# Gated linear attention: the first 512 tokens in plain float32, batch 0's softmax over q on TensorE, and a new order of steps

## The chip, the cores and the metric

The kernel runs on one core of one Trainium2 chip. The metric is the device time of one execution in microseconds (us), median of the runs shown; lower is better.

## The reference

Batch B = 8, heads H = 8, sequence S = 576, head width D = 64, so the model width is C = 512. Cut to what matters:

```
q_s = softmax(q, over the 64 channels of a head)          # one group per token and head
k_s = softmax(k, over the 576 tokens)                      # one group per head and channel
kv  = k_s^T v                                              # 64 x 64 per head
x   = q_s kv                                               # 576 tokens x 512 channels per batch
gate = sigmoid(conv_w, 5 causal taps over the tokens, of x)
out = ((gate * (x @ w_val)) @ w_out)                       # both weights 512 x 512
```

`w_val`, `conv_w` and `w_out` come as 64-bit floats, and the kernel itself turns their two 32-bit words into float32.

## The kernel before, in words

The whole kernel is one list of steps, `ORDER`, written out by hand; each name in it is a function, and every engine's queue holds its instructions in just that order (PE is TensorE, DVE is VectorE, ACT is ScalarE, POOL is GpSimd; SP issues every DMA). A letter at the end of a step (`a`, `v`, `p`) says which engine does it: ACT, DVE or POOL. A step whose input isn't there holds up everything behind it on its engine.

The weights: `load_words i` brings one slab of 128 columns (0 to 3 of `w_val`, 4 to 7 of `w_out`, 8 the taps); `field`, `part`, `scaled`, `signed`, `joined` make float32 of it (L235 to L254); `w_high` rounds it to float32r, and `w_low` takes the rest (L256 to L262).

Per batch b: `load_q`, `q_max`, `q_sub`, `q_exp`, `q_sum`, `q_mul` are the softmax over q with tokens on the partitions (L377 to L393); `q_turn` transposes it on PE (L399), and `q_turned` copies it to `qT`, channels on the partitions. Batches 0 to 2 go this way; later ones load q transposed and take a log-sum through memory. `k_top`, `k_raise`, `k_turn`, `k_turned` are the softmax over k for batches 0 and 1. `kv b` (40 calls of a float32 matmul in 128x64 and 64x64 tiles, L463) and `kv_norm` give `kvd`; `attend b g` (8 calls, 288 columns each, two token halves by two head pairs by two row halves, so four 64x64 tiles of the array at once, L492) writes x of two channel blocks p = 2g, 2g+1 to PSUM. There are two such PSUM tiles (tag `x`, two banks each), so `attend b 1` waits until every reader of `attend b 0` is done. The readers are `first` and four `tap`s per block (the convolution; on DVE in one instruction, L528, or as an ACT product and a POOL add, L532 and L533), `x_high` (x rounded to float32r, into `xx`) and `x_low` (the rest, L514). `sigmoid` is a tanh on ACT.

Then the 4608 tokens are cut in nine tiles of 512, i = 0 to 8; tile 0 is the first 512 tokens of batch 0. `value i m` is 128 rows of x @ w_val in 12 float32r matmuls of 512 columns (three products of high and low halves for each of four blocks, L549); `gated` multiplies with the gate, `g_high` and `g_low` split the product, and `project i t` is another 12 matmuls (L573); `store` evicts and writes. Four `value` and four `project` steps stand for each tile, 72 in all:

```
for kb in range(NB):
    hi, lo = T["xx", i, kb][:, :C], T["xx", i, kb][:, C:]
    for j, (a, z) in enumerate(((wl, hi), (wh, hi), (wh, lo))):
        nc.tensor.matmul(ps, a[:, kb, ms], z, start=(kb == 0 and j == 0), stop=(kb == NB - 1 and j == 2))
```

Other PSUM results use four banks of tag `mm`. The functions of the diff follow.

Of the kernel before, what the change touches and what calls it, by code (L numbers as in the profile page):

```python
# [37 lines left out]
PITCH = 2340  # L38
GAPS = {'w': 64, 'pair': 96, 'gp': 96}

ORDER = [step.strip() for step in """
    load_words 8, field 8, part 8 a, load_q 0 r, scaled 8 v, signed 8, q_max 0 r, q_sub 0 3 v, q_sub 0 2 p, q_exp 0 r,
    joined 8 p, load_q 0 l, q_max 0 l, load_words 0, field 0, q_sub 0 0 v, scaled 0 a, load_q 1 a, part 0 a,
    load_words 3, part 3 a, q_sub 0 1 v, signed 0, joined 0 p, load_kc 0 2, q_sum 0 r, load_ident, field 3, scaled 3
    a, load_kc 0 0, load_kc 0 3, load_kc 0 1, load_words 4, q_max 1 a, w_high 0 a, q_exp 0 l, load_words 2, k_top 0 3,
    k_raise 0 3, k_top 0 1, k_raise 0 1, k_turn 0 1, q_mul 0 2 p, q_mul 0 3 p, q_tail_turn 0, k_top 0 0, k_top 0 2,
    k_raise 0 2, k_raise 0 0, k_turn 0 2, w_low 0 p, q_sum 0 l, k_turned 0 2 a, k_tail_turn 0, q_tail_turned 0 a,
    field 2, load_v 0, field 4, scaled 4 a, q_sub 1 1 v, q_sub 1 3 p, q_mul 0 1 v, part 2 a, signed 4, k_turn 0 0,
    signed 3, load_kc 1 1, k_turned 0 0 a, q_sub 1 0 p, q_sub 1 2 p, scaled 2 a, signed 2, k_turn 0 3, joined 2 p,
    k_turned 0 1 a, k_tail_turned 0 a, k_turned 0 3 a, kv 0, load_kc 1 0, q_exp 1 a, q_mul 0 0 v, q_turn 0 0,  # L50
    load_words 1, w_high 2 p, q_turned 0 0 a, k_top 1 1, kv_norm 0 0 a, q_turn 0 1, q_turned 0 1 a, field 1, scaled 1
    a, q_sum 1 a, joined 3 p, w_high 3 a, q_turn 0 2, q_turned 0 2 a, w_low 2 p, attend 0 0, first 0 1 a, x_high 0 1 0
    a, load_q 5 a, first 0 0 a, q_turn 0 3, kv_norm 0 1 a, x_high 0 0 1 a, load_kc 1 2, k_top 1 2, k_raise 1 2, tap 0
    1 0 v, w_low 3 p, x_high 0 1 1 a, q_mul 1 0 p, part 4 a, joined 4 p, tap 0 0 1 a, load_words 5, load_words 6, part
    5 a, w_high 4 a, field 5, scaled 5 a, field 6, signed 1, tap 0 1 1 v, w_low 4 p, q_turned 0 3 a, q_mul 1 1 p,
    k_raise 1 1, q_mul 1 3 p, load_kc 1 3, k_top 1 3, x_low 0 1 0, x_low 0 1 1, part 1 a, q_mul 1 2 v, q_turn 1 0, tap
    0 1 3 a, tap 0 0 0 v, load_q 2 a, x_high 0 0 0 a, load_words 7, q_max 2 a, field 7, q_sub 2 3 p, k_turn 1 2,
    q_turned 1 0 a, load_km 2 0, scaled 6 a, x_low 0 0 0, k_turned 1 2 a, tap 0 0 3 v, x_low 0 0 1, q_turn 1 1, k_turn
    1 1, k_raise 1 3, q_turn 1 3, k_turned 1 1 a, k_turn 1 3, load_km 2 1, tap 0 0 2 v, sigmoid 0 0, signed 5, joined
    5 p, load_v 1, q_sub 2 0 p, scaled 7 a, q_tail_turn 1, q_turned 1 1 a, q_tail_turned 1 a, load_qc 5, w_high 5 a,  # L60
    k_top 1 0, k_raise 1 0, tap 0 1 2 v, k_peak 2 0, attend 0 1, k_peak 2 1, x_high 0 2 0 a, k_turn 1 0, load_k 4,
    x_high 0 3 0 a, x_low 0 3 0, first 0 2 a, k_turned 1 0 a, x_high 0 3 1 a, q_turn 1 2, q_turned 1 2 a, k_tail_turn
# [586 lines left out]
```

## Time and profile before

| | |
|---|---|
| median of 3 runs | 297.15 us (296.78 to 297.23) |
| profiled execution | 297.07 us, span 295.3 us |
| PE busy | 261.6 us, 89% of the span |
| DVE busy | 244.8 us, 83% |
| ACT busy | 192.4 us, 65% |
| POOL busy | 195.8 us, 66% |

A row of a view gives a start, a busy time and the instruction's tile names (output <- inputs). Busy times of neighbours overlap a little, so the cost of an instruction in a full queue is the distance from its start to the next start. Matmuls overlap by more, and for them only distances of starts count. The granted clock is the share of TensorE's full 2.4 GHz.

### The profile page before, as it was taken

The numbers are of one execution on the slowest core, as the hardware profiler recorded it, in microseconds if no ns is written. First come the engines' busy times: TensorE is split into PE (matmuls) and PEld (weight loads), VectorE is DVE, ScalarE is ACT, GpSimd is POOL, SyncE is SP. The second block draws the span as 40 slices with busy tenths as digits, with TensorE's granted clock in tenths as the row PEclk, the third lists the DMA queues.
The fourth block names the chain that finished last, engine by engine and source line by source line (L and its number), as shares of the span: only waits on it lengthen the run. The fifth ranks groups of instructions, "written<-read, shape, count | busy, mean of one in ns | idle before, by whom it ended". The sixth has DMA issues, their size and how long they took to land.

```text
span 295.3 us, 5125 instructions
## 1 busy us (share of the span) xinstructions
PE 261.6 (89%) x1854; PEld 202.9 (69%) x1854; DVE 244.8 (83%) x412; ACT 192.4 (65%) x299; POOL 195.8 (66%) x184
## 2 busy tenths in 40 slices
...
GB/s 230 386 406 406 356 252 366 385 285 271 269 283 232 220 259 211 299 198 243 228 199 169 159 309 296 188 108 271 237 127 228 2 71 78 29 2 0 107 90 88
DMA packets 21801, 63.06 MB, mean 214 GB/s; under 512 B 3472, under 2 KB 7696, under 8 KB 18448
## 3 DMA queue, kind: packets, MB, share of 16 engines
...
## 4 chain that ended last, share of the span: by engine, by line
PE 80%; DVE 8%; ACT 3%; POOL 3%; DMA 2%; issue 1%; SPq 0%; DVEq 0%; POOLq 0%; ACTq 0%
PE val L549 32%; PE out L573 31%; PE kv L463 7%; PE x L492 6%; DMA words<-in_w_val 2%; PE kps L326 2%; DVE gate L528 2%; PE qps L399 1%; DVE g L556 1%; DVE gl L564 1%; DVE kpk L282 1%; DVE qm L377 1%; ACT qT L194 1%; POOL gl L564 1%; ACT gate L520 1%
## 5 line engine op out<-in xcount | busy, mean ns | idle before, releaser
L549 PE MATMUL val<-xx,w_val_hi 128*128 128x512 f32 x288 | 88.9, 390 | 0.0
L533 POOL TENSOR_TENSOR gate<-gate,far 128x572 f32<-128x572 f32 (+3 forms) x46 | 58.7, 1280 | 33.7 <-ACT far L532 32.1
L528 DVE SCALAR_TENSOR_TENSOR gate<-x,cw,gate 128x574 f32<-128x574 f32 (+3 forms) x82 | 65.3, 806 | 0.8
L549 PEld LDWEIGHTS val<-xx,w_val_hi 128*128 128x128 f32 x288 | 54.1, 188 | 11.0
L573 PE MATMUL out<-w_out_hi,gl 128*128 128x512 f32 x144 | 56.7, 394 | 1.4 <-DVE gl L564 1.1
L549 PE MATMUL val<-xx,w_val_lo 128*128 128x512 f32 x144 | 57.7, 400 | 0.3 <-DVE g L556 0.3
L573 PE MATMUL out<-w_out_lo,gh 128*128 128x512 f32 x144 | 57.4, 399 | 0.2 <-ACT gh L194 0.2
L573 PE MATMUL out<-w_out_hi,gh 128*128 128x512 f32 x144 | 56.2, 390 | 0.0
L532 ACT ACTIVATE far<-x,cw 128x572 f32<-128x572 f32 (+3 forms) x46 | 33.5, 747 | 15.2 <-DVE gate L528 7.2
L564 POOL TENSOR_TENSOR gl<-g,gh 128x512 fp32r<-128x512 f32 x26 | 28.8, 1113 | 14.3 <-ACT gh L194 9.5
L380 POOL TENSOR_TENSOR q<-q,qm 128x576 f32<-128x576 f32 x27 | 32.6, 1226 | 5.9 <-DVE qm L377 5.9
L556 DVE SCALAR_TENSOR_TENSOR g<-gate,val 128x128 f32<-128x128 f32 (+7 forms) x64 | 27.4, 447 | 8.9 <-PE val L549 5.9
L549 PEld LDWEIGHTS val<-xx,w_val_lo 128*128 128x128 f32 x144 | 27.0, 188 | 9.5 <-issue 3.1
L573 PEld LDWEIGHTS out<-w_out_hi,gl 128*128 128x128 f32 x144 | 27.0, 188 | 9.3 <-DVE gl L564 1.9
L573 PEld LDWEIGHTS out<-w_out_lo,gh 128*128 128x128 f32 x144 | 27.0, 188 | 9.0 <-issue 3.1
L514 DVE TENSOR_TENSOR xx<-x,xx 128x512 fp32r<-128x512 f32 (+7 forms) x64 | 27.5, 449 | 5.4 <-ACT xx L194 4.0
L573 PEld LDWEIGHTS out<-w_out_hi,gh 128*128 128x128 f32 x144 | 27.0, 188 | 5.3
L200 ACT ACTIVATE o<-out 128x512 f32<-128x512 f32 x25 | 14.8, 599 | 21.6 <-PE out L573 21.6
L194 ACT CAST xx<-x 128x448 fp32r<-128x448 f32 (+7 forms) x39 | 15.7, 414 | 14.7 <-PE x L492 7.9
L538 ACT ACTIVATE gate<-gate 128x576 f32<-128x576 f32 x32 | 21.5, 684 | 5.8 <-DVE gate L528 2.8
L326 PE MATMUL kps<-ident,kc 128*128 128x128 f32 x32 | 8.0, 408 | 18.3 <-ACT kc L214 18.3
L520 ACT ACTIVATE gate<-x,cw 128x576 f32<-128x576 f32 x23 | 16.9, 746 | 9.7 <-DVE xx L196 5.4
...
## 6 DMA issues: line engine op xcount, KB each, us to landing
...
```

What stands on the lines that cost most here:

```text
L380: engine(e).tensor_sub(groups(b, h), groups(b, h), wide(T["qm", b], h))
L463: nc.tensor.matmul(to, kk[r, o:o + D], vv[r, c * H + n], start=(c == 0), stop=(c == 4))
L514: nc.vector.tensor_sub(xx(i, p)[:, n], T["x", b, p][:, t], xx(i, p)[:, o].bitcast(F32))
L520: nc.scalar.activation(a, x, AF.Copy, scale=w)
L528: nc.vector.scalar_tensor_tensor(out=a, in0=x, scalar=w, in1=a, op0=ALU.mult, op1=ALU.add)
L532: nc.scalar.activation(part, x, AF.Copy, scale=w)
L533: nc.gpsimd.tensor_add(a, a, part)
L538: nc.scalar.activation(T["gate", b, p], T["gate", b, p], AF.Tanh, scale=0.5)
L549: nc.tensor.matmul(ps, a[:, kb, ms], z, start=(kb == 0 and j == 0), stop=(kb == NB - 1 and j == 2))
L556: nc.vector.scalar_tensor_tensor(out=T["g", i, m][:, o], in0=T["gate", b, m][:, t], scalar=1.0, in1=T["val", i, m][:, o], op0=ALU.add, op1 ...
L564: engine(e).tensor_sub(T["gl", i, m], T["g", i, m], T["gh", i, m].bitcast(F32))
L573: nc.tensor.matmul(ps, a, z[:, kb], start=(kb == 0 and j == 0), stop=(kb == NB - 1 and j == 2))
```

## The change

- The constant `ident` becomes 258 columns wide: the identity, its negative, and two columns that sum 64 rows each (`pairs_of`). It is loaded first.
- Batch 0's softmax over q: `q_lift` brings raw q across with a matmul by the identity, `q_lower` subtracts the row maxima (the maxima spread over 64 columns, times the negative identity, accumulated in the same PSUM tile), `q_raise` is the exponential out of PSUM into `qT`; `q_total` sums over channels by a matmul with two columns, `q_rate` inverts, `q_wide` spreads the inverses over channels by matmul, `q_scale` multiplies. This takes the place of `q_sub`, `q_exp`, `q_sum`, `q_mul`, `q_turn`, `q_turned` for batch 0. These PSUM tiles use tag `x`.
- `heat` and `warm` are transposes of the identity whose results nobody reads.
- Tile 0: `value 0 m` and `project 0 t` use the float32 weights (`wp`) and float32 x and g in 4 matmuls each, in place of 12 float32r ones; `x_low` of tile 0 and `g_high`, `g_low` of tile 0 go.
- The weights stand in 18 slots of tag `w` (8 `wp`, 8 `wh`, 8 `wl` in all), slabs of `w_out` are now rows, not columns, and the `w_high`, `w_low` steps come later in the order. `q_sum` no longer inverts; `q_inverse` does for batches 1 and 2.
- `GAPS` changes, and `ORDER` is new throughout.

The diff, cut to its core (the new order up to the first projections; the rest of the orders left out):

```diff
+PITCH = 2340
+GAPS = {'pair': 16, 'gp': 112}
...
-PITCH = 2340
-GAPS = {'w': 64, 'pair': 96, 'gp': 96}
+WS = 18
...
+    load_ident, heat 0 0, heat 1 0, load_words 8, field 8, scaled 8 a, signed 8, part 8 p, load_q 0 l, q_max 0 l, heat
+    2 16, heat 3 0, load_q 0 r, q_max 0 r, q_lift 0 1, q_lower 0 1, load_q 1 a, q_lift_end 0, q_lower_end 0,
+    load_words 7, q_raise 0 1, load_kc 1 1, q_lift 0 3, q_lower 0 3, q_lift 0 0, q_max 1 a, q_raise_end 0, field 7,
+    scaled 7 a, load_kc 0 2, k_top 0 2, k_top 1 1, q_lower 0 0, q_lift 0 2, q_lower 0 2, part 7 a, q_sub 1 1 p, q_sub
+    1 0 p, k_raise 0 2, q_sub 1 2 p, k_raise 1 1, joined 8 p, load_kc 0 1, k_top 0 1, q_sub 1 3 p, q_raise 0 0,
+    load_words 4, part 4 a, field 4, scaled 4 a, load_kc 0 0, load_kc 0 3, k_top 0 0, k_raise 0 0, signed 7, load_kc 1
+    2, q_raise 0 2, k_top 1 2, q_raise 0 3, warm 0 8, q_total 0 0, q_total 0 1, q_total 0 2, load_words 3, k_top 0 3,
+    q_total 0 3, q_total_end 0, signed 4, field 3, q_exp 1 a, load_words 2, field 2, k_turn 0 0, k_turned 0 0 a,
+    scaled 2 p, warm 1 4, warm 2 8, load_kc 1 0, q_rate 0, q_wide 0 0, k_raise 0 1, k_turn 0 1, k_raise 0 3, scaled 3
+    a, k_tail_turn 0, part 2 a, q_wide 0 1, q_sum 1 a, joined 4 p, warm 3 0, load_words 0, field 0, warm 4 8, q_scale
+    0 0, part 0 a, q_inverse 1 a a, k_turned 0 1 a, q_scale 0 1, load_kc 1 3, k_top 1 3, signed 3, scaled 0 a, k_turn
+    0 3, load_v 0, part 3 a, q_mul 1 3 p, load_words 6, field 6, k_turn 0 2, k_turned 0 2 a, load_km 2 0, k_raise 1 3,
+    q_wide_end 0, k_tail_turned 0 a, k_top 1 0, k_turned 0 3 a, load_words 5, q_scale_end 0, q_wide 0 2, q_scale 0 2,
+    kv 0, k_peak 2 0, k_raise 1 0, joined 3 p, k_raise 1 2, kv_norm 0 0 a, field 5, scaled 5 a, w_high 3 a, kv_norm 0
+    1 a, load_q 2 a, q_wide 0 3, q_scale 0 3, q_mul 1 0 p, signed 0, q_mul 1 1 p, warm 5 4, attend 0 0, first 0 1 a,
+    first 0 0 a, q_mul 1 2 p, q_turn 1 1, signed 2, load_km 3 1, joined 2 p, load_words 1, tap 0 1 2 v, tap 0 0 2 a,
+    load_km 2 1, x_high 0 0 1 a, tap 0 1 0 a, q_max 2 a, q_sub 2 0 p, tap 0 0 0 v, joined 0 p, k_tail_turn 1, k_turn 1
+    0, k_turned 1 0 a, q_turned 1 1 a, x_high 0 1 0 a, q_tail_turn 1, x_low 0 0 1, q_tail_turned 1 a, tap 0 1 3 v,
+    scaled 6 a, k_turn 1 2, tap 0 0 1 v, part 1 a, load_v 1, load_v 3, k_tail_turned 1 a, x_high 0 1 1 a, x_low 0 1 1,
+    k_turn 1 3, k_turned 1 3 a, tap 0 0 3 v, k_turned 1 2 a, x_high 0 0 0 a, k_turn 1 1, k_turned 1 1 a, q_turn 1 2,
+    tap 0 1 1 v, q_turn 1 0, q_turned 1 0 a, q_sub 2 2 p, w_high 4 a, signed 6, signed 5, part 5 a, q_turn 1 3, part 6
+    a, q_turned 1 3 a, field 1, joined 5 p, attend 0 1, first 0 3 a, x_high 0 2 0 a, joined 6 p, scaled 1 a, kv 1,
+    k_peak 2 1, tap 0 3 2 v, load_q 3 a, load_v 2, first 0 2 a, x_high 0 3 0 a, kv_norm 1 0 a, tap 0 2 3 v, tap 0 2 1
+    v, value 0 2, sigmoid 0 0, value 0 0, k_row 2, q_sub 2 3 p, q_sub 2 1 p, q_exp 2 a, signed 1, x_high 0 2 1 v,
...
     def w_high(i, e="a"):
-        copied(e, W[i // NB][0][:, :, slab(i)], T["f", i].bitcast(F32).rearrange("p (k c) -> p k c", k=NB))
+        copied(e, weight("wh", i, F32R), T["wp", i].bitcast(F32))
...
+    def heat(k, n):
+        for j in range(n):
+            nc.tensor.transpose(zone(0, 0)[:, j % 2 * P:j % 2 * P + P], ident, ident)
+
+    def q_lift(b, p):
+        for c in range(4):
+            o = c * C + p * P
+            nc.tensor.matmul(zone(b, p)[:, c * P:(c + 1) * P], T["q", b][:, o:o + P], ident, start=(c == 0), stop=False)
...
+    def over_heads(to, t, o, by, start, stop):
+        for h in range(2):
+            w = t[:, o + h:o + h + 1].broadcast_to([P, D])
+            nc.tensor.matmul(to[h * D:(h + 1) * D], w, by, start=start, stop=stop)
+
+    def q_lower(b, p):
+        for c in range(4):
+            over_heads(zone(b, p)[:, c * P:(c + 1) * P], T["qm", b], c * H + 2 * p, minus, False, c == 3)
...
+    def q_raise(b, p):
+        exp(across(b)[:, p, :MAIN], zone(b, p))
...
+    def q_total(b, p):
+        for c in range(4):
+            o = c * H + 2 * p
+            nc.tensor.matmul(totals(b)[:, o:o + 2], across(b)[:, p, c * P:(c + 1) * P], pairs_of, start=True, stop=True)
...
+    def q_wide(b, p):
+        for c in range(4):
+            over_heads(zone(b, p, "rate")[:, c * P:(c + 1) * P], T["qs", b], c * H + 2 * p, ident, True, True)
...
+    def q_scale(b, p):
+        t = across(b)[:, p, :MAIN]
+        nc.vector.tensor_mul(t, t, zone(b, p, "rate"))
...
     def value(i, m):
         ps = T["val", i, m] = bank(f"val_{i}_{m}")
...
+        if i == 0:
+            w = cols(T["wp", m].bitcast(F32))
+            for kb in range(NB):
+                nc.tensor.matmul(ps, w[:, kb], T["xx", i, kb][:, :C], start=(kb == 0), stop=(kb == NB - 1))
+            return
...
     def project(i, t):
         ps = T["out", i, t] = bank(f"out_{i}_{t}")
...
+            if i == 0:
+                nc.tensor.matmul(ps, T["g", i, kb][:, ts], T["wp", NB + kb].bitcast(F32), start=(kb == 0), stop=(kb == NB - 1))
+                continue
```

## Rows read from the trace of the kernel before

**Rows 1.** The page, busy time of each engine with share and instructions.
```profile
PE 261.6 (89%) x1854; PEld 202.9 (69%) x1854; DVE 244.8 (83%) x412; ACT 192.4 (65%) x299; POOL 195.8 (66%) x184
```

**Rows 2.** The page, the chain that ended last, shares by engine.
```profile
PE 80%; DVE 8%; ACT 3%; POOL 3%; DMA 2%; issue 1%; SPq 0%; DVEq 0%; POOLq 0%; ACTq 0%
```

**Rows 3.** Windows: stretch, length, busy of PE, PEld, DVE, ACT, POOL; clock, DMA, GB/s.
```profile
0.00:18.29 18.29, 0.00 (x0) 0.00 (x0) 13.49 (x21) 7.98 (x11) 8.07 (x13) 1.00 0.90 327
18.29:30.50 12.21, 11.97 (x134) 9.43 (x134) 11.94 (x22) 10.98 (x20) 6.52 (x7) 1.00 1.04 408
30.50:38.89 8.39, 0.33 (x2) 0.14 (x1) 8.31 (x16) 7.96 (x17) 6.78 (x7) 0.72 0.71 265
38.89:44.42 5.53, 5.53 (x26) 5.20 (x26) 5.50 (x10) 4.94 (x10) 4.39 (x4) 0.50 0.91 338
44.42:49.05 4.63, 3.41 (x29) 1.93 (x28) 4.63 (x6) 4.46 (x10) 4.63 (x6) 1.00 0.96 356
49.05:87.98 38.93, 38.77 (x335) 30.01 (x337) 38.30 (x57) 33.41 (x56) 35.41 (x36) 1.00 0.86 305
87.98:291.31 203.33, 201.55 (x1337) 156.17 (x1336) 162.69 (x286) 122.05 (x178) 130.05 (x118) 1.00 0.58 168
```

**Rows 4.** The chain in order of time: start, length, what, with the matmul records.
```profile
52.08 2.83 PE kv L463 x80
...
60.58 1.13 PE x L492 x16
...
247.07 22.20 PE val L549 x96
```

**Rows 5.** Timeline of PE: start, busy time, instruction and how many.
```profile
28.42 1.50 PE L492 MATMUL x<-qT,kvd 64*64 64x288 f32 x16
...
64.49 1.04 PE L399 MATMUL qps<-ident,q 128*128 128x128 f32 x8
65.36 0.38 PE L413 MATMUL qtps<-ident,q 128*128 128x128 f32 x2
```

**Rows 6.** Timeline of DVE, a first wait and a stretch without idle time.
```profile
4.96 1.35 DVE L377 TENSOR_REDUCE qm<-q 128x18 f32<-128x1152 f32 x1 [1.75 <-DMA q<-in_q]
...
37.42 2.53 DVE L377 TENSOR_REDUCE qm<-q 128x36 f32<-128x2304 f32 x1
39.88 0.41 DVE L242 TENSOR_SCALAR e<-words 128x512 f32<-128x512 f32 x1
40.22 0.68 DVE L514 TENSOR_TENSOR xx<-x,xx 128x512 fp32r<-128x512 f32 x1
40.82 0.80 DVE L528 SCALAR_TENSOR_TENSOR gate<-x,cw,gate 128x575 f32<-128x575 f32 x1
41.54 0.20 DVE L514 TENSOR_TENSOR xx<-x,xx 128x64 fp32r<-128x64 f32 x1
...
42.40 0.41 DVE L249 TENSOR_SCALAR e<-e 128x512 int32<-128x512 int32 x1
...
43.45 0.74 DVE L317 TENSOR_REDUCE ktop<-kc 128x1 f32<-128x576 f32 x1
44.11 0.80 DVE L528 SCALAR_TENSOR_TENSOR gate<-x,cw,gate 128x574 f32<-128x574 f32 x1
```

**Rows 7.** Timeline of ACT, two instructions of a full stretch.
```profile
30.12 0.74 ACT L520 ACTIVATE gate<-x,cw 128x576 f32<-128x576 f32 x1
30.76 0.58 ACT L194 CAST xx<-x 128x512 fp32r<-128x512 f32 x1
```

**Rows 8.** Timeline of POOL, two splits of a weight slab.
```profile
29.04 2.15 POOL L262 TENSOR_TENSOR w_val_lo<-f,w_val_hi 128x512 fp32r<-128x512 f32 x2
```

**Rows 9.** Waits: who for whom, total us, times, longest.
```profile
PE out L573 <- DVE gl L564: 1.1, 2, 0.6
```

**Rows 10.** Windows of PE alone: stretch, length, busy, granted clock, DMA share, GB/s.
```profile
23.95:34.19 10.24, 6.64 (x107) 1.00 1.03 404
34.19:44.43 10.24, 5.54 (x26) 0.50 0.71 255
```

More of the change, by code (lines that the diff above doesn't have):

```diff
@@ new lines @@
+    1 a, q_sum 2 a, sigmoid 0 1, load_k 3, tap 0 2 2 v, q_inverse 2 a a, q_mul 2 0 p, joined 7 p, q_mul 2 1 p, tap 0 3
+    3 v, sigmoid 0 3, x_low 0 2 1, w_high 1 a, kv_norm 1 1 a, q_max 3 a, value 0 3, gated 0 3 0, attend 1 0, value 0
+    1, q_mul 2 2 p, q_mul 2 3 p, q_turn 2 0, load_k 2, first 1 0 a, tap 1 0 0 a, q_sub 3 2 p, w_high 6 p, x_high 1 0 0
+    v, x_low 1 0 0, load_km 4 0, sigmoid 0 2, gated 0 2 0, gated 0 0 0, x_high 1 1 0 a, w_low 1 p, q_turn 2 3, first 1
+    1 a, tap 1 1 0 a, x_high 1 0 1 a, x_high 1 1 1 v, q_turned 2 0 a, q_turn 2 2, gated 0 1 0, q_turned 2 3 v, tap 1 0
@@ new lines @@
+    1 v, project 0 1, k_peak 3 1, q_tail_turn 2, tap 1 0 3 v, q_turned 2 2 a, q_turn 2 1, x_low 1 1 0, tap 1 1 1 v,
+    load_km 3 0, q_turned 2 1 a, load_qc 3, x_low 1 0 1, tap 1 1 2 v, tap 1 1 3 v, q_sub 3 3 p, load_km 4 1, q_sub 3 0
+    p, q_sub 3 1 p, tap 1 0 2 v, x_low 1 1 1, k_sub 2 4 p, k_peak 4 0, store 0 1 a, k_sub 2 2 p, project 0 2, q_exp 3
+    a, k_peak 3 0, k_row 3, w_high 0 a, w_low 4 p, attend 1 1, first 1 2 a, k_sub 2 0 p, load_qc 5, x_high 1 3 1 a,
+    k_sub 2 3 p, k_sub 2 1 p, project 0 3, q_sum 3 a, w_high 7 p, w_low 7 p, tap 1 2 1 a, k_peak 4 1, project 0 0,
@@ new lines @@
+    store 0 2 a, k_spread 3, x_high 1 3 0 a, w_low 0 p, first 1 3 a, tap 1 3 1 v, sigmoid 1 0, x_low 1 3 0, w_high 5
+    a, x_high 1 2 0 a, q_tail_turned 2 v, x_low 1 2 0, value 1 1, w_low 6 p, q_max 4 a, q_sub 4 1 p, w_low 5 p, store
+    0 3 a, k_exp 2, x_high 1 2 1 v, kv 2, tap 1 2 2 v, tap 1 2 3 v, x_low 1 2 1, load_q 5 a, x_low 1 3 1, tap 1 3 2 v,
+    tap 1 3 0 v, w_high 2 p, q_log 3, q_level 3 p, q_row 3, store 0 0 a, tap 1 3 3 v, load_km 5 0, w_low 2 p, sigmoid
+    1 1, kv_norm 2 0 a, value 1 0, tap 1 2 0 v, attend 2 0, sigmoid 1 2, w_low 3 p, value 1 2, gated 1 1 1, gated 1 1
@@ new lines @@
+    0, g_high 2 2 a, x_high 3 1 1 a, g_low 2 2 p, x_high 3 0 1 a, gated 2 3 1, g_high 2 3 a, tap 3 1 3 v, g_low 2 3 v,
+    q_spread 4 1, x_high 3 0 0 a, project 2 1, tap 3 0 2 a, q_exp 5 a, tap 3 1 0 v, x_low 3 0 0, store 2 1 a, x_low 3
+    1 1, q_spread 4 0, project 2 0, kv_norm 3 1 v, sigmoid 3 0, store 2 0 a, x_low 3 0 1, attend 3 1, x_high 3 2 1 a,
+    x_high 3 3 0 a, k_sub 4 4 p, q_max 6 a, k_sub 4 3 p, q_sub 6 3 v, load_q 7 a, q_sub 6 2 p, q_sub 6 1 p, first 3 3
+    a, tap 3 3 3 v, x_high 3 2 0 a, x_low 3 2 0, project 2 3, x_low 3 2 1, tap 3 3 1 a, x_low 3 3 0, first 3 2 a,
```

330 lines of the change are left out of this document (189 added, 141 removed).

## Prediction

> **What bounds the kernel now.** The busy times come first: PE 89% of the span, DVE 83% [rows 1], and the chain that ended last runs 80% on PE [rows 2]. A share over the whole span says nothing of the stages, so the windows are next [rows 3]. From 49.05 to 291.31 us PE is busy without a gap worth naming (38.77 of 38.93, 201.55 of 203.33). Before 49.05 it is not: nothing until 18.29, then 12 us of work, a hole of 8 us, and 5.5 us at half clock. In those first 49 us DVE is the full engine (11.94 of 12.21, 8.31 of 8.39, 5.50 of 5.53, 4.63 of 4.63), and it still is in the next stage (38.30 of 38.93). So the end is the moment at which PE becomes full, plus the PE work that is then left, plus 4 us of last store. The change can act on three things: DVE's work in the first 49 us (gain), PE's work after it (loss), and new waits.
>
> **PE: plain float32 in tile 0.** A step of 12 float32r matmuls costs 22.20 / 8 = 2.78 us [rows 4]. No row has a float32 matmul of the full array with 512 columns, so I bound it. Transposes are float32 and cost 0.87 us for 8, so 109 ns for 128 columns, with one record per call [rows 5]; by that, 4 calls of 512 columns cost 4 x 0.436 = 1.74 us. `attend` is 8 calls by its code but 16 records: each float32 call runs twice. Four tiles go at once, so 1.13 us [rows 4] holds two rounds, and a call of 288 columns costs at most 0.565 us, 1.96 ns a column with filling; 4 calls of 512 would be 4.0 us. Two records at the transposes' pace (0.85 ns a column each) make 0.87 us a call, 3.49 us a step, and they explain `attend` too (4 x 0.245 = 0.98 us plus filling). I take 3.49, nearer to the row that is an ordinary product. Eight steps: 8 x (3.49 - 2.78) = +5.7 us of PE work; the ends are -8.3 and +9.8 us.
>
> **DVE: what goes.** A tap costs 0.72 us, `q_max` of a batch 2.46, a 512-wide `x_low` 0.60, a `signed` 1.05, a `k_top` 0.66, a `field` 0.34, all as distances of starts [rows 6]. Tile 0 loses four `x_low` (-2.4). Batch 0's q loses three `q_sub` and two `q_mul` on DVE (5 x 0.68, the distance being that of a 576-wide operation without the tap's scalar, bounded by 0.60 and 0.72) and `q_sum` (2.46), and gains four `q_scale` of 512 out of PSUM (0.60 as `x_low`, 0.72 at most) and about 0.5 for the ends: -3 us. ACT and POOL lose `q_exp`, `q_turned`, `g_high`, `g_low` and get `q_raise`; the `w_high` and `w_low` (1.08 us each on POOL [rows 8]) are only moved behind the first values.
>
> **The start, step by step.** DVE's queue up to `q_scale 0 3`, behind which `attend 0 0` has to wait (its second PSUM tile is the slot of the second rate tile): 7 fields and the taps' 2.6, three `signed` and the taps' 3.5, `q_max` of batches 0 and 1 4.9, `q_sum 1` 2.5, eight `k_top` 5.3, `q_scale` 2.9, `q_rate`, `q_inverse`, two `kv_norm` 1.4 (short ones, estimated), `k_peak` 1.3 (half a `q_max`): 24.4 us. Its idle time: the first half of q came at 4.96 [rows 6] with only the taps ahead, now 0.13 MB of constants are ahead too, 0.4 us at 327 GB/s [rows 3]; so 5.3, of which 0.8 is used by the taps' fields. At the same pace the second half lands at 7.2 and batch 1's q at 10.7, which leaves holes of 0.7 and 2.3 us; with small ones 7.9 us. So `q_scale 0 3` ends at 32.3, and `attend 0 0` starts there: 3.9 us later than now (28.42 [rows 5]). Under that cover lie: the lifts and lowers on PE (16 rounds of 128 float32 columns and the ends, 7.7 us at full clock, 15 at half, between 7.2 and `q_raise` of the last block, which waits for `k_raise 0 0` on ACT until about 18); `q_total`, 20 calls bound by their weight loads (two at the transposes' 109 ns each, 4.4 us); `q_wide` (0.9 us each); and v of batch 0, now the nineteenth load of SP's queue behind 7.5 MB: 6.0 MB are there at 18.29, the rest and its own 1.2 MB come at 408 GB/s [rows 3] by 25, and `kv 0` needs 2.83 us [rows 4]. If that cover went, v is late first: each us beyond 28 would be paid in full.
>
> From 32.3: `attend 0 0` 1.3, `first` 0.64 [rows 7], then DVE has six taps, one `q_max` and two narrow `x_low` before the x tiles are free: 4.3 + 2.5 + 0.3 = 7.1, so 41.3 (two `signed` lie under `attend`). ACT's list up to the last `x_high` is of equal length: four products and copies of x at 0.64 each, eight copies and exponentials of 0.5 [rows 7], and short ones, 7.6 us from 33.6. `attend 0 1` starts at 41.4, against 44.42 now [rows 3]. It takes 1.5 and `kv 1` 2.8, while ACT does two `first`, two `x_high` and a `scaled` (2.8): the first `value` starts at 46.0, with `kv 1` done. Now it starts at 49.05, with `kv 1` still to do.
>
> **The sum.** From 46.0 to `attend 2 0` PE has eight float32 steps 27.9, two `attend` 2.3, 18 transposes 2.0, `value 1 1` and `value 1 0` 5.9 with the change of type, `kv 2` 2.8: 40.9 us, so 86.9. Now that point is 87.98: -1.1 us. DVE's queue for the same stretch, counted the same way, is 36 us and 2 us of lag, below 40.9, so PE stays the bound. Behind it PE's work is the same in both. Of PE's waits there 1.1 us are for DVE's `g_low` [rows 9]; DVE now has about 7 us less behind it at the same point of PE, and I take these off: -2.2 us. The profiled execution took 297.07 us with a span of 295.3, so **294.9 us**; the median shown is 0.08 above that execution.
>
> **The rivals.**
> *PE enters the first value at half clock* (slower or no change). The granted clock fell at 34.19 after PE had hardly worked since 30.5, and rose at 44.43 after 5.5 us of unbroken work [rows 3, 10]. In the new order PE has some 36 transposes (4 us) in the 8 us before `attend 0 1`. If the clock is down there, 5.5 us of work cost twice as much, +2.7 us: 297.6. For it: the hole is as sparse as the one before. Against it: at half clock the same transposes fill the hole (7.7 of 8 us) and so end it early. It decides if the clock is still half when `kv 1` starts. The Trainium skill ("TensorE: Matmul & The Clock Gate", Part 4: PE-mode transpose) says that transposes don't count as activity towards the full clock; by that rule `warm` and `heat` would do nothing, the rise would come only behind `attend 0 1`, and 297.6 would be the time. The trace speaks against it: the rise at 44.43 follows 26 transposes and nothing else [rows 3].
>
> *POOL becomes the bound* (slower). The moved `w_low`s fall in the stage where POOL is already busy 35.41 of 38.93 us [rows 3]; 18 slots for 24 weight tiles keep the last six from being made before tile 0 has read its plain weights. Eight splits are 8.6 us, the removed `g_low`s and the q steps moved forward about as much. If three splits come late, `value 1 2` or `value 1 3` waits 3 x 1.08 = 3.2 us: 298.1. It decides if `w_low 3` isn't done when `value 1 2` ends, near 91 us.
>
> *Float32 runs at the transposes' pace* (faster): PE loses 8.3 us instead of gaining 5.7, but then DVE's 38 us are the bound up to `attend 2 0`: about 84, so 3 us more: 291.9. Against it: two records a call.
>
> **The numbers.** Forecast 0.57, clock 0.20, POOL 0.17, cheap float32 0.06. A difference under 0.2% (0.6 us) is what a measurement here can hardly tell from none. The forecast rests on idle time and landing times that can be off by 3 us: its own range is 291.9 to 297.5, with 0.53 faster and 0.04 within 0.2%. The clock's case, paid in part or in full, gives 0.03 faster, 0.07 same, 0.10 slower; POOL's 0.02 same and 0.15 slower; cheap float32 0.06 faster. Together faster 0.62, same 0.13, slower 0.25. The range reaches from the cheap float32 to POOL's case: 291.5 to 298.3.
>
> **What would show it.** Right: `value 0` in 8 records, about 0.43 us apart; first `value` near 46 with `kv 1` before it; `attend 0 0` later than 28.42 and `attend 0 1` near 41; `attend 2 0` near 87; DVE's busy time down by some 8 us. Wrong: a granted clock of 0.5 behind 42 us; PE waiting on a POOL split between 80 and 95; a value step of 1.7 or 4.0 us; v landing after 28.

## The result, and the profile after

The changed kernel takes 299.95 us (median of 4 runs, 299.22 to 301.51) against 297.19 (4 runs, 296.78 to 297.35): a ratio of 1.010, 95% interval 1.0079 to 1.0121. It is 1% slower; 294.9 was forecast. The profiled execution took 300.3 us with a span of 298.5. Medians below are over all runs of a kernel; ratios leave out runs more than 1.5% above the kernel's fastest, so the two need not agree. Each ratio is to the kernel before, run beside it. In what follows, lifts, lowers, totals and spreads are the steps `q_lift`, `q_lower`, `q_total` and `q_wide`, turns are `k_turn`, and dummies are the transposes of `warm`.

The page of the changed kernel, busy times (engine, us, share of the span, instructions), answers to [rows 1]:

```profile
PE 287.4 (96%) x2072; PEld 217.6 (73%) x2072; DVE 236.6 (79%) x397; ACT 186.1 (62%) x291; POOL 185.6 (62%) x180
```

PE is busy 25.8 us longer, DVE 8.2 us less. The windows, cut at the same events as in [rows 3] (start of `attend 0 0`, `attend 0 1`, the first `value`, `attend 2 0`):

```profile
0.00:18.20 18.20, 15.18 (x135) 13.52 (x135) 10.29 (x14) 7.16 (x12) 5.49 (x11) 1.00 0.89 318
18.20:36.13 17.93, 17.93 (x236) 16.25 (x237) 14.29 (x29) 12.73 (x23) 7.80 (x7) 0.90 1.05 416
36.13:46.33 10.20, 8.12 (x58) 6.01 (x61) 10.10 (x16) 9.39 (x22) 7.32 (x7) 0.83 1.00 400
46.33:50.18 3.85, 3.85 (x98) 2.96 (x97) 3.82 (x6) 3.85 (x8) 2.04 (x2) 1.00 0.46 191
50.18:90.94 40.76, 40.76 (x222) 21.71 (x225) 39.13 (x59) 29.94 (x49) 37.71 (x37) 1.00 0.79 257
90.94:294.65 203.71, 201.56 (x1337) 157.13 (x1336) 158.95 (x277) 122.47 (x181) 125.25 (x118) 1.00 0.54 169
```

The columns are length, busy time of PE, weight loads, DVE, ACT, POOL, then granted clock, DMA share, GB/s. Before, PE did nothing until 18.29 and DVE was full; now PE is busy 17.93 of 17.93 us up to `attend 0 0`, and DVE only 14.29. So PE is the new full engine of the start, and `attend 0 0` comes 3.8 us later than forecast. From the first `value` to `attend 2 0` it is 40.76 us (forecast 40.9).

PE's timeline of the start (start, busy, line, output <- inputs, count; waits in brackets):

```profile
6.49 2.09 PE L421 MATMUL zone<-ident,q 128*128 128x128 f32 x8
...
16.07 1.09 PE L431 MATMUL zone<-ident,qm 128*64 128x128 f32 x16
17.10 1.09 PE L601 MATMUL x<-ident 128*128 128x128 f32 x8
18.03 3.63 PE L461 MATMUL total<-ident,qT 128*128 128x2 f32 x32
21.59 0.41 PE L467 MATMUL total<-ident,qT 128*64 128x2 f32 x8
21.93 1.03 PE L337 MATMUL kps<-ident,kc 128*128 128x128 f32 x4
22.76 2.77 PE L601 MATMUL x<-ident 128*128 128x128 f32 x12
25.45 1.09 PE L431 MATMUL rate<-ident,qs 128*64 128x128 f32 x16
...
27.50 1.09 PE L431 MATMUL rate<-ident,qs 128*64 128x128 f32 x16
```

and DVE's at the same place:

```profile
22.30 0.38 DVE L472 RECIPROCAL qs<-qs 128x36 f32<-128x36 f32 x1
22.59 2.50 DVE L398 TENSOR_REDUCE qs<-q 128x36 f32<-128x2304 f32 x1
25.00 0.41 DVE L252 TENSOR_SCALAR e<-words 128x512 f32<-128x512 f32 x1
28.64 0.69 DVE L484 TENSOR_TENSOR qT<-qT,rate 128x512 f32<-128x512 f32 x1 [3.23 <-PE rate L431]
...
35.91 0.67 DVE L484 TENSOR_TENSOR qT<-qT,rate 128x512 f32<-128x512 f32 x1
```

PE goes from lifts and lowers through dummies and totals to the spreads without a gap. DVE has the rates ready at 22.7 us, but PE still runs a k block and 12 dummy transposes until 25.45; DVE stands 3.23 us until the second spread is written. From there DVE is the full engine again: its first and its last `q_scale` start 7.27 us apart without a wait between them, and `attend 0 0` follows. This repeats: in the changed kernel and eleven of the runs below the first `q_scale` starts 0.05 to 0.11 us behind the end of the second spread, the last one 7.25 to 7.27 us later, and `attend 0 0` 7.2 to 7.5 us behind the first. So PE's queue counts up to the second spread (28.6 us in the changed kernel); the 12 dummies behind it lie under DVE's queue.

One thing more is in these rows. The first `q_scale` reads only what the first spread wrote, and that was done at 26.54; but both spreads write the two halves of one PSUM tile, and in `ORDER` the first `q_scale` stands behind both. No run puts it ahead of the second spread, so how much of the 3.23 us this order costs was not tried.

The clock of the same stretch (length, PE busy, granted clock, DMA share, GB/s):

```profile
18.20:22.00 3.80, 3.80 (x40) 1.00 1.08 393
22.00:23.00 1.00, 1.00 (x6) 0.53 1.14 463
23.00:25.50 2.50, 2.50 (x14) 0.51 1.00 419
25.50:28.60 3.10, 3.10 (x42) 1.00 1.02 418
```

It fell near 22.0, with PE busy all the time but on two-column products, and so the twelve dummies behind them run at half clock: 2.69 us from start to start, not 1.3. It rose again near 25.5.

### The profile page after: what moved, and what is told of

The parts are those of the page before. It is cut to its first block, busy times and chain, and to the rows that moved or that the text cites. A ratio compares the mean times of both kernels' runs of the same rounds, so it can differ in the third digit from the quotient of the medians.

```text
span 298.5 us, 5518 instructions
## 1 busy us (share of the span) xinstructions
PE 287.4 (96%) x2072; PEld 217.6 (73%) x2072; DVE 236.6 (79%) x397; ACT 186.1 (62%) x291; POOL 185.6 (62%) x180
## 4 chain that ended last, share of the span: by engine, by line
PE 79%; DVE 10%; DMA 4%; ACT 3%; POOL 2%; issue 1%; DVEq 0%; ACTq 0%
PE out L742 23%; PE val L712 22%; PE kv L569 7%; PE x L610 6%; PE val L706 5%; PE out L737 5%; DVE gate L686 4%; DMA q<-in_q 3%; PE x L601 2%; PE zone L421 2%; DVE g L722 2%; DVE qm L388 2%; PE qps L505 1%; PE zone L431 1%; POOL q L391 1%; PE rate L431 1%
## 5 line engine op out<-in xcount | busy, mean ns | idle before, releaser
L712 PE MATMUL val<-xx,wh 128*128 128x512 f32 x256 | 79.0, 390 | 0.0
L686 DVE SCALAR_TENSOR_TENSOR gate<-x,cw,gate 128x572 f32<-128x572 f32 (+3 forms) x90 | 71.7, 807 | 3.2 <-ACT gate L678 2.3
L691 POOL TENSOR_TENSOR gate<-gate,far 128x574 f32<-128x574 f32 (+3 forms) x38 | 46.0, 1213 | 28.1 <-ACT far L690 26.2
L712 PEld LDWEIGHTS val<-xx,wh 128*128 128x128 f32 x256 | 48.1, 188 | 10.1 <-issue 0.2
L712 PE MATMUL val<-xx,wl 128*128 128x512 f32 x128 | 51.3, 401 | 0.4 <-DVE g L722 0.2
L742 PE MATMUL out<-wl,gh 128*128 128x512 f32 x128 | 50.9, 397 | 0.0
L742 PE MATMUL out<-wh,gl 128*128 128x512 f32 x128 | 50.1, 391 | 0.6 <-DVE gl L730 0.6
L742 PE MATMUL out<-wh,gh 128*128 128x512 f32 x128 | 49.9, 390 | 0.0
L690 ACT ACTIVATE far<-x,cw 128x574 f32<-128x574 f32 (+3 forms) x38 | 27.8, 745 | 11.4 <-DVE gate L686 7.6
L202 ACT ACTIVATE o<-out 128x512 f32<-128x512 f32 x31 | 18.2, 595 | 22.7 <-PE out L742 15.1
L696 ACT ACTIVATE gate<-gate 128x576 f32<-128x576 f32 x32 | 22.1, 692 | 11.1 <-DVE gate L686 9.3
L672 DVE TENSOR_TENSOR xx<-x,xx 128x64 fp32r<-128x64 f32 (+7 forms) x60 | 25.3, 434 | 3.5 <-ACT xx L196 2.7
```

What stands on the lines that cost most here:

```text
L672: nc.vector.tensor_sub(xx(i, p)[:, n], T["x", b, p][:, t], xx(i, p)[:, o].bitcast(F32))
L686: nc.vector.scalar_tensor_tensor(out=a, in0=x, scalar=w, in1=a, op0=ALU.mult, op1=ALU.add)
L690: nc.scalar.activation(part, x, AF.Copy, scale=w)
L691: nc.gpsimd.tensor_add(a, a, part)
L696: nc.scalar.activation(T["gate", b, p], T["gate", b, p], AF.Tanh, scale=0.5)
L712: nc.tensor.matmul(ps, a[:, kb], z, start=(kb == 0 and j == 0), stop=(kb == NB - 1 and j == 2))
```

## The experiments

The theories: the loss is the start's, where PE's in-order queue holds DVE up (the queue theory, Q in the texts); DVE's own order is at fault (W); the half clock behind the totals is the price (the clock theory); loads or DVE set `attend 0 0`, and PE's queue costs nothing (D). The rival: plain float32 costs more than the 5.7 us forecast, or DVE's relief pays for part of it.

**The dummies: none, not even their tile, double.** Edits in `ORDER`:

```
-warm 0 8, warm 1 4, warm 2 8, ...
+warm 0 0, warm 1 0, warm 2 0, ...        (first run: tile taken, no transposes)
+                                          (second run: steps left out)
+warm 0 16, warm 1 8, warm 2 16, ...      (third run)
```

> The changed kernel with its 32 warm transposes left out (their PSUM tile is still taken at the same place). Theory Q (PE's own queue from 17 to 36 us, full in the trace after, sets attend 0 0): the transposes took 1.03 + 2.56 + 1.02 + 0.59 = 5.2 us of that queue, so attend 0 0 comes at 31 to 33 us instead of 36.1, allowing up to 2 us back for products that then run at the half clock, and the time falls from 300.0 to 296 to 297.5 us. Theory D (loads or DVE set attend 0 0, the transposes only fill a wait): attend 0 0 stays within 0.5 us of 36.1 and the time within 0.6 us of 300.

> The changed kernel without the warm steps at all, so that the x tile isn't taken before attend 0 0 and the second rate tile need not wait for the first one's readers. Theory Q: as with the transposes alone left out, 296 to 297.5 us, and up to 1 us less where q_wide 0 2 no longer waits for q_scale 0 1. Theory D: within 0.6 us of 300.

> The changed kernel with 64 warm transposes in place of 32. Theory Q: 5.2 us more in a full queue, less what a higher clock gives back, attend 0 0 at 39 to 41 us and the time 303 to 305 us. Theory D: they fill waits, the time rises by less than 1.5 us.

Measured: 298.92 us, ratio 1.0063 (1.0031 to 1.0095); 298.58, 1.0053 (1.003 to 1.0077); 304.70, 1.0234 (1.0178 to 1.0289). Double costs 4.75 us and puts `attend 0 0` 3.4 us later, so PE's queue is on the path. Leaving out gives only 1.0 and 1.4 us of 5.2, the first at the edge of the noise, and `attend 0 0` hardly moves (35.87 and 35.91). PE's timeline without the transposes shows why:

```profile
22.82 1.98 PE L431 MATMUL rate<-ident,qs 128*64 128x128 f32 x16 [1.13 <-DVE qs L472]
24.73 1.12 PE L337 MATMUL kps<-ident,kc 128*128 128x128 f32 x4
25.63 1.06 PE L350 MATMUL ktps<-ident,kc 128*128 128x128 f32 x4
26.62 1.97 PE L431 MATMUL rate<-ident,qs 128*64 128x128 f32 x16
```

The first spread starts 2.6 us earlier, but both spreads and the turns between them run at half clock (1.98 us for 1.09), and DVE's `q_scale` starts at 28.64, as in the changed kernel. The first spread also waits 1.13 us for `q_rate`, which DVE's order holds at 22.07.

**No `heat` ahead of the first q.**

```
-heat 2 16
+heat 2 0
```

> The changed kernel without the 16 heat transposes at the start. Theory Q: lifts and lowers begin no sooner (they wait for q) but run at half clock until about 5.4 us of work are done, so 2 to 3 us are lost before q_total and the time is 302 to 303 us. Theory D: no change within 0.6 us of 300. If transposes didn't raise the clock, there would be no change either, and lifts would show the same pace in both.

Measured: 302.16 us, 1.0109 (1.0074 to 1.0145), from 298.19 us in a run at a granted clock of 1.000 to 303.77 in ten runs. The ratio is that of the changed kernel (1.0100), so the 302 to 303 expected is not borne out clear of the spread. The paces differ, though: in the profiled run the first lower takes 1.98 us, in the changed kernel 1.09; PE comes to the pace of the full clock near 12.0 us without the 16 transposes and near 8.5 us with them.

**DVE's order.**

```
-q_scale 0 0, ..., q_inverse 1 a a, ..., load_kc 1 3, k_top 1 3, signed 3
+q_inverse 1 a a, load_kc 1 3, k_top 1 3, signed 3, q_scale 0 0
```

> The changed kernel with one k_top, one signed and the inverse of batch 1 put ahead of the first q_scale in DVE's queue. Theory W (DVE's 3.2 us of waiting for the first q_wide is what put attend 0 0 behind the forecast): 2 of the 3.2 us are filled, attend 0 0 comes 1.5 to 2 us earlier and the time falls to 298 to 298.7 us. Rival (loads of k or PE set attend 0 0, DVE's wait is idle time without a price): no change within 0.6 us of 300.

Measured: 301.81 us, 1.0116 (1.0057 to 1.0176). No gain; filling DVE's wait with other work does not move the spread it waits for. This order does not help, but its four runs lie 4.8 us apart, at granted clocks of 0.975 to 0.993, so it settles little.

**Plain float32 alone**, in the order and with the softmax of before (the weights' tiles and slabs are those of the changed kernel, with 21 slots):

```
+if i == 0:
+    for kb in range(NB): nc.tensor.matmul(ps, w[:, kb], T["xx", i, kb][:, :C], start=(kb == 0), stop=(kb == NB - 1))
-x_low 0 0 0, ..., g_high 0 0 a, g_low 0 0 p, ...
```

> The order and the softmax of the kernel before, with only tile 0 in plain float32 (no x_low, g_high, g_low of tile 0; 21 weight slots). PE theory: eight steps cost 0.72 us more each, 5.7 us in a stage where PE is full, less 1 to 2 us for the earlier first value: 300.5 to 302 us. DVE theory (DVE is the real limit up to 98 us and its 2.4 us fewer are worth more than PE's 5.7): 295 to 298 us.

Measured: 303.08 us against 297.33, 1.0213 (1.0181 to 1.0245): +5.75 us (5.4 to 7.3 by the interval), against the PE sum's +5.7. Four calls are eight records:

```profile
56.15 7.13 PE L705 MATMUL val<-xx,wp 128*128 128x512 f32 x16
...
64.34 3.70 PE L705 MATMUL val<-xx,wp 128*128 128x512 f32 x8
```

The rival falls: the step costs what the sum says, and DVE's relief pays for none of it; the first `value` came at 49.80, 0.75 us later than in the kernel before.

**The new softmax and order with float32r in tile 0.** To have its halves in time, each weight's split stands right behind `joined`.

> The changed kernel with tile 0 back in three float32r products: x_low of tile 0, its g_high and g_low, and all weight splits are put back into the new order, each behind the step that makes its input. PE theory: eight steps of 0.72 us less, and the first value later by what the splits add on ACT and POOL, which are half idle there: 295 to 297 us. DVE theory: DVE gets 2.4 us more, the time stays at 300 or above.

Measured: 324.71 us, 1.0919 (1.086 to 1.0978). A miss: the early splits hold up the start. Waits of PE (waiting op <- releaser: us, times, longest):

```profile
PE kps L339 <- ACT k L198: 8.3, 1, 8.3
PE qps L507 <- POOL q L501: 3.0, 2, 1.7
```

So it does not price the softmax alone.

**Sums spread by one wide product per block**, reciprocal on DVE behind it, product on POOL, no `warm`:

```
+nc.tensor.matmul(zone(b, p, "rate"), heads_of, across(b)[:, p, :MAIN], start=True, stop=True)
+nc.vector.reciprocal(r, zone(b, p, "rate"))
+nc.gpsimd.tensor_mul(t, t, r)
```

> The changed kernel with the sums of batch 0's softmax made spread out at once: four float32 matmuls of 512 columns with a matrix of ones per head, the inverse on DVE and the product on POOL, in place of q_total, q_rate, q_wide and q_scale, and no warm steps. Theory W: the chain through q_total (2-column products), q_rate and q_wide is gone, DVE has no 3 us wait, attend 0 0 comes at 31 to 33 us instead of 36 and the time is 295 to 297 us, at or below the kernel before. Rival (v or k of batch 0 arrives too late): kv 0 still starts at 31 to 32, attend 0 0 stays near 35 to 36, and the time is 298.5 to 300.

Measured: 311.0 us, 1.0456 (1.0434 to 1.0478). The sums were there early, but the reciprocal was mis-sized. DVE's timeline:

```profile
22.11 6.56 DVE L487 RECIPROCAL inv<-rate 128x512 f32<-128x512 f32 x2
...
32.77 6.55 DVE L487 RECIPROCAL inv<-rate 128x512 f32<-128x512 f32 x2
```

3.28 us for 512 columns, against 0.38 for the 36 columns of the changed kernel (22.30 above).

**A rearranged start with the totals spread, and the same with the totals together.**

```
+... q_lift 0 0, ..., q_total 0 1, ..., q_lift 0 2, q_total_end 0, ..., q_lower 0 2, q_total 0 3, ...   (first)
+... q_total 0 1, q_total_end 0, q_total 0 3, q_total 0 0, q_total 0 2, q_rate 0, ...                   (second)
```

> The order without the dummy transposes, with the steps ahead of attend 0 0 rearranged: each q_total stands behind the next lift instead of all five together, the spreads and q_scale follow at once, the k transposes lie between them, v of batch 0 is loaded earlier, and 14 steps that attend 0 0 does not need (fields, signs and maxima of later weights and of batch 1's k) go behind it. Computes the same. If the start is set by PE's own queue, and the clock falls because the two-column products stand together: the granted clock stays 1.0 from the lifts to the k transposes, the first q_scale starts near 22 to 24 us instead of 28.6, attend 0 0 near 31 to 33 (now 35.9), attend 0 1 near 43 to 44 (its DVE work stays, less 3.2 us of idle time), first value near 47, total 295.0 to 296.5. If landing times of k's channels, words or v set the start: attend 0 0 stays near 36 and the total near 298.6, and the waits in front of it name a DMA. If the DVE work that was moved behind attend 0 0 is what counts: attend 0 0 earlier, but attend 0 1 still at 46 and the total near 298.6.

> As the run with the totals between the lifts, but the five q_total steps stand together in front of q_rate, 4 us of two-column products without anything else. Computes the same. If such a stretch is what lets the clock fall: the granted clock is 0.5 for 3 to 7 us behind it, attend 0 0 is 2 to 3 us later than in the other run, and the total 0.5 to 2.5 us above it. If the clock falls for another reason (or not at all in either): both runs have the same clock and differ by no more than the 1 us by which the later sums can delay the rates.

Measured: 315.73 us, 1.0618 (1.0592 to 1.0645), and 318.32, 1.0692 (1.0669 to 1.0714). Both miss by far: with signs, fields and maxima put behind the scales, DVE stands at the rate and at each scale with nothing else in front. DVE's timeline of the first:

```profile
23.02 0.20 DVE L471 TENSOR_SCALAR qs<-total 128x36 f32<-128x36 f32 x1 [5.78 <-PE total L461]
...
29.96 1.28 DVE L484 TENSOR_TENSOR qT<-qT,rate 128x512 f32<-128x512 f32 x2 [5.71 <-PE rate L431]
...
37.38 1.28 DVE L484 TENSOR_TENSOR qT<-qT,rate 128x512 f32<-128x512 f32 x2 [5.09 <-ACT q L216]
```

Between the two, the clock fell about 1 us sooner with the totals together (mean grant in 21 to 23 us 0.76 against 1.00), which fits the clock theory; a later run does not.

**PE's queue cut: no `q_lower`; then no maxima and no dummies either.**

```
-start=(c == 0), stop=False)          # q_lift
+start=True, stop=True)
-q_lower 0 1, q_lower_end 0, q_lower 0 3, q_lower 0 0, q_lower 0 2
-q_max 0 l, q_max 0 r, warm ...       (second run only)
```

The last lift and the exponentials also stand earlier, right behind the other lifts.

> The changed kernel without the matmuls that subtract the maxima in batch 0's q (q_lower, 4.7 us of PE's queue); the softmax is then taken without a shift. The maxima are still formed on DVE, the dummy transposes stay, the lifts end at once, and the exponentials stand right behind the lifts on ACT. DVE's queue and the loads are as they were. If PE's own queue sets the start: DVE's wait of 3.2 us for the first spread goes, attend 0 0 comes at 32.5 to 33.5 (36.1 in the changed kernel, 32.3 in the forecast), attend 0 1 at 43 to 44, the total 296 to 297.5. If DVE's queue or the landing of loads sets it: attend 0 0 stays within 0.7 us of 36.1 and the total at 299 to 300.

> As the run without q_lower, and also without the maxima of batch 0 on DVE (q_max, 2.8 us) and without the dummy transposes (5.2 us of PE's queue). The softmax of batch 0's q is taken without a shift. If PE's queue alone set the start, the maxima are worth nothing and the total is that of the run without q_lower, or 1 us less for the dummies, unless the clock falls in the emptier start: then the spreads take 2 us instead of 1 and the total is equal or higher. If DVE becomes the bound as soon as PE's queue is shorter (the forecast's sum): 2 to 3 us less than the run without q_lower, 293.5 to 295.

Measured: 297.55 us, 1.0002 (0.9983 to 1.0021), and 299.70, 1.0089 (1.0064 to 1.0115). 4.7 us out of PE's queue are worth 2.4, but not in the way that the text above names: `attend 0 0` comes at 35.25 in place of 32.5 to 33.5, and DVE still waits 2.64 us for the second spread, because the totals, begun at 14.11, run at half clock from near 16 us (5.37 us busy for 3.63). In the profiled run 0.9 us is gained there, the first `value` comes 1.2 us earlier, and a wait of 1.1 us far behind (named below) is gone. 8.0 us more out of the two queues (5.2 PE, 2.8 DVE) make it worse. In the second, PE is ahead of DVE's list:

```profile
12.16 5.59 PE L460 MATMUL total<-ident,qT 128*128 128x2 f32 x32 [1.18 <-ACT qT L215]
17.68 0.60 PE L466 MATMUL total<-ident,qT 128*64 128x2 f32 x8
18.21 1.12 PE L336 MATMUL kps<-ident,kc 128*128 128x128 f32 x4
22.22 1.98 PE L430 MATMUL rate<-ident,qs 128*64 128x128 f32 x16 [2.88 <-DVE qs L471]
```

The totals are done at 18.3 us, at half clock, and then wait for `q_rate`, which stands behind a `signed` and two fields in DVE's queue. That is a third cause, its own run below.

**Dummies between the totals**, without `q_lower` (four behind each total, 24 ahead of the spread) and in the changed kernel (two behind each):

```
-warm 0 8, q_total 0 0, q_total 0 1, ...
+q_total 0 0, warm 10 2, q_total 0 1, warm 11 2, ...
```

> The run without q_lower, with its eight dummy transposes ahead of the totals replaced by four behind each of the four q_total steps, and 24 instead of 12 ahead of the first spread; the softmax is taken without a shift. DVE's queue is the same. If the clock falls because two-column products stand together: it stays at 1.0 up to the first spread, the two spreads take 1.02 us each instead of 1.97 and 1.02, the first q_scale starts near 25.5 to 26 (27.84 there), attend 0 0 near 33 (35.25), total 295.5 to 296.5. If the clock falls at that time whatever PE does: half clock from about 16 us again, the 24 dummies cost 5 us and the total is 299 or more.

> The changed kernel with the same number of instructions: the eight dummy transposes that stood ahead of the totals go two behind each q_total. If they keep the clock up: no fall at 22 us, the twelve dummies behind take 1.3 instead of 2.6 us, attend 0 0 at 34.5 to 35 (36.1), total 298.3 to 299. If not: as the changed kernel, 299.5 to 300.3.

Measured: 299.30 us, 1.0012 (0.9979 to 1.0045), and 299.87, 1.0055 (1.0029 to 1.0082). Neither is a cure: in the profiled runs the clock falls as before, and most other runs have as low a mean grant. Over the runs of these two kernels the time tends to go with the granted clock. First kernel: three runs at 0.998 to 0.999 took 295.81 to 296.06 us, five at 0.982 to 0.987 took 298.29 to 299.56. Second: the run at 1.000 took 296.87, one at 0.994 took 298.23, five at 0.985 to 0.987 took 299.01 to 299.88. By these a granted clock of 0.985 goes with some 3 us more than one near 1. That is a comparison of runs and not an experiment, and the clock does not explain all: one run at 0.991 took 301.13, eight more of the two kernels at 0.977 to 0.987 took 300.80 to 302.49, and the changed kernel's own four runs do not follow it (299.22 at 0.986, 301.51 at 0.989). (The kernel before, beside them, ran at 0.980 to 0.988 and took 296.84 to 298.67 in 29 runs.)

**`q_rate` early**, no `q_lower`, no dummies but two behind each total:

```
-signed 4, field 3, ..., field 2, ..., q_rate 0
+q_rate 0, signed 4, field 3, ..., field 2
```

> The run without q_lower, with q_rate ahead of a signed and two fields in DVE's queue (1.9 us of it) and with no dummies but two behind each q_total; the softmax is taken without a shift. If the start is the chain totals, rate, spreads, q_scale and DVE's place in it: q_rate starts at 20 instead of 21.9, the first q_scale finds its spread done or waits less than 1 us (2.64), attend 0 0 at 32.5 to 33.5, total 295.5 to 296.5. If the landing of k's channels, words or v sets it: attend 0 0 stays at 35 and the total at 297.5.

Measured: 296.37 us (294.92 to 299.07, 12 runs), 0.9973 (0.9945 to 1.0001). It is the only kernel with a median below the one before; its interval still takes in 1, and it leaves out the subtraction of the maxima. Its 12 runs all have a granted clock of 0.981 to 0.987 and yet lie 4 us apart. The profiled run took 295.37; its windows up to the first `value` (same columns):

```profile
0.00:32.73 32.73, 27.68 (x273) 24.89 (x273) 24.75 (x41) 19.85 (x33) 13.03 (x18) 0.84 0.95 364
32.73:42.68 9.95, 7.11 (x55) 4.71 (x55) 9.88 (x16) 9.17 (x22) 7.59 (x7) 1.00 1.03 419
42.68:46.62 3.94, 3.94 (x96) 3.23 (x96) 3.87 (x8) 3.94 (x8) 1.62 (x2) 1.00 1.05 436
```

`attend 0 0` is at 32.73 us, 0.4 behind the forecast's 32.3, with no DVE wait on PE, although the clock is 0.84.

**The whole softmax without `q_lower`:** maxima subtracted ahead of the lifts.

```
+q_max 0 l, q_sub 0 0 v, q_sub 0 1 p, ..., q_max 0 r, q_sub 0 2 v, q_sub 0 3 p
```

> As the run with q_rate early, but the whole softmax is computed: the maxima are subtracted in q before the lifts, two quarters on DVE (0.7 us each) and two on POOL (1.15 us each), in place of the 4.7 us of q_lower on PE. If PE's queue was the price, moving this to engines that are idle then is worth nearly what leaving it out is: DVE 1.4 us longer, of which 1.4 us of its wait for batch 1's q can take most, the lifts end 2 to 3 us later than without the subtraction; attend 0 0 at 33 to 34.5, total 296 to 297.2, at or just below the kernel before. If DVE is the bound of the start, as the forecast had it: 1.4 us more than the run without the subtraction in full.

Measured: 301.60 us, 1.0147 (1.0121 to 1.0172). A miss: the lifts now wait for each subtraction (PE is busy 3.92 of the 7.00 us from 5 to 12), the granted clock is 0.83 there, 0.66 up to 18.5 and 0.59 up to 31 us, and `attend 0 0` comes at 39.01.

```profile
8.22 0.49 PE L421 MATMUL zone<-ident,q 128*128 128x128 f32 x2 [1.80 <-DVE q L391]
9.23 0.49 PE L421 MATMUL zone<-ident,q 128*128 128x128 f32 x2 [0.52 <-POOL q L391]
...
18.51 1.05 PE L461 MATMUL total<-ident,qT 128*128 128x2 f32 x8 [1.18 <-ACT qT L216]
```

**All computed, few dummies; and totals between lifts, no dummies.**

```
-warm 0 8, warm 1 4, warm 2 8, warm 3 0, warm 4 8, warm 5 4
+q_total 0 0, warm 10 2, ..., q_total 0 3, warm 13 2                                         (first)
+q_lower 0 0, q_total 0 1, ..., q_total 0 3, q_lower 0 2, ..., q_total 0 0, ..., q_total 0 2, q_rate 0   (second)
```

> The changed kernel with only eight dummy transposes, two behind each q_total; the 24 others are left out. Computes the same. PE's queue: 22 us up to q_rate as before, then 2.6 us less ahead of the first spread and 1.6 us less behind it. If the queue is what counts: the first q_scale at 25.9 to 27 (28.64 in the changed kernel), attend 0 0 at 33.5 to 35, total 297 to 298.5. If the clock takes it back, as in the run without any dummies: half clock from 22 to 29, attend 0 0 near 36, total 298.6 or more.

> The order without dummy transposes, with the q_total steps put between the lifts and lowers as their exponentials come ready (and these ahead of a scaled and k's exponentials on ACT), and q_rate ahead of two fields on DVE; nothing else is moved. Computes the same. If the start is PE's queue up to the rates and the clock on the way: the totals end at 21.3 instead of 22.0, the clock does not fall before 23, the spreads take 1.0 to 1.4 us, the first q_scale starts at 25 to 26, attend 0 0 at 32.7 to 33.7, total 295.5 to 297. If the clock falls in 22 to 25 anyway: the spreads take 2 us each, attend 0 0 at 34.5 to 35.5, total 297.3 to 298.5. If landing sets the start: attend 0 0 at 36, total 298.6.

Measured: 298.82 us, 1.0048 (1.0018 to 1.0079), and 300.40, 1.0105 (1.0073 to 1.0137). The first is like leaving out all dummies: the clock is at 0.50 from 21.6 to 27.5 us, and `attend 0 0` comes at 35.79. The second is a miss, and against the strict form of the clock theory, in which only totals that stand together let the clock fall. Its windows (length, PE busy, granted clock, DMA share, GB/s):

```profile
15.00:18.00 3.00, 3.00 (x34) 1.00 1.05 391
18.00:19.00 1.00, 1.00 (x12) 0.76 1.08 381
19.00:24.00 5.00, 4.75 (x28) 0.50 1.09 420
```

The totals began at 15.07 with lifts and lowers between them; the clock fell in the middle of a `q_lower`, with PE busy throughout, 3.5 us sooner than in the changed kernel. The clock is not all of this miss: ACT stood 4.50 us until 20.28 in front of the last exponential of q, the `scaled` behind it came late, DVE waited 3.39 us for that one and made the rates from 24.93, not 22.07; `attend 0 0` comes at 37.57.

## Why the forecast was wrong, point by point

The last column is from a profiled run 1 us below its kernel's median.

| | before | forecast | changed | `q_rate` early |
|---|---|---|---|---|
| `attend 0 0` | 28.42 | 32.3 | 36.13 | 32.73 |
| `attend 0 1` | 44.42 | 41.4 | 46.33 | 42.68 |
| first `value` | 49.05 | 46.0 | 50.18 | 46.62 |
| `attend 2 0` | 87.98 | 86.9 | 90.94 | 87.48 |
| from there to PE's end | 203.33 | 202.2 | 203.7 | 202.2 |

- **float32, +5.7 us: right.** 3.50 us a step (10.50 for three), 437 ns a record; alone it costs 5.75.
- **DVE's queue up to `attend 0 0`, 24.4 us: right.** 10.29 + 14.29 = 24.58 us busy up to 36.13; 24.75 in the run with `q_rate` early.
- **DVE's idle time, 7.9 us, and "Under that cover lie": the step that failed.** It is 36.13 - 24.58 = 11.5 us. I took DVE's queue for the bound and hid PE's new chain beneath it, item by item, never adding up PE's own queue in order. From the first lift at 6.49 us to the end of the second spread at 28.59, from which DVE's last 7.3 us start, it holds lifts and lowers 10.6 us (I had 7.7), eight dummies 0.9, totals 3.9 (4.4), the first turn 0.8, twelve dummies 2.7 at half clock, the two spreads 2.1 and the turns between them 1.0: 22.1 us without a gap. The dummies, 3.6 us of it, and the turns were not in my list. One wait of 3.23 us for the second spread is nearly the whole difference. With PE's queue shorter and `q_rate` ahead, idle time is 32.73 - 24.75 = 8.0 us, as forecast, and the later points lie within 1.3 us of it.
- **From the first value to `attend 2 0`, 40.9 us: right** (40.76).
- **Stalls, -1.1 us behind `attend 2 0`: not realized.** PE's end came 203.7 us after it, 1.5 more than forecast. The wait for `g_low` shrank from 1.1 to 0.6 us and did not vanish, and a new wait of 1.1 us stands in the list of waits of the changed kernel:

```profile
PE kv L569 <- DVE kpk L293: 1.1, 1, 1.1
```

The chain in time leads to it from a load of q that began at 123.55 us (9.44 us), through its maximum and POOL's subtractions. In the run with `q_rate` early the wait is gone and the stretch is 202.2 us. The early start as such is not the reason: with the maxima subtracted ahead of the lifts `attend 0 0` comes at 39.01, and the wait is gone and the stretch 202.3 all the same; with few dummies it comes at 35.79, and the wait is there and the stretch 204.0. What decides it stays open.

Together: 90.94 - 86.9 = 4.0 us and 1.5 us make 300.3, the profiled time, from 294.9 (with 0.1 in the last store).

**The rivals.** The clock's place was wrong: `kv 1` and the first `value` ran at full clock (1.00 in 46.33:50.18). The half clock came earlier, in the start: 3.5 us of PE's work ahead of the second spread ran at it (22.0 to 25.5), which is 1.75 us lost in this trace; runs compared by their granted clock differ by about 3. It came again ahead of `attend 0 1` (0.50 from 43 to 45 us), where I had looked for it, but the stretch from `attend 0 0` to there is only 0.25 us longer than at full clock in the run with `q_rate` early (10.20 and 9.95), and it ended before `kv 1`. POOL is not the bound (no wait of PE names it), and float32 isn't cheap. "Slower" came by none of the mechanisms to which I gave a chance.

What stays open: the 3.2 us wait hangs on dummies, lowers, half clock, `q_rate`'s place and the first `q_scale`'s place behind both spreads at once, and the last was not tried. Taking out 4.7 us of PE's work gave 2.4 us (0.9 of it at `attend 0 0`), `q_rate`'s place with fewer dummies 1.2, which is within the noise of the two; a granted clock near 1 went with about 3. They overlap and do not add. No kernel here that computes the whole softmax this way beats the one before.
